# Two edits to a fused attention and two-MLP kernel: the activation's coefficients handled in the planned order, and the last output rows in two halves

## The chip, the core and the metric

The kernel runs as one program on one core of a Trainium2 chip. The time of a run is the device time in microseconds (us). Five engines work side by side, each through its own queue in order: TensorE (PE, whose weight loads are listed as PEld), VectorE (DVE), ScalarE (ACT), GpSimd (POOL) and SyncE (SP), which here only issues DMAs. A DMA can also be issued from ACT's queue. An instruction that has to wait holds up everything behind it on its engine.

## The reference, cut to what matters

Attention over 2 batches of 768 positions with 8 heads of 64 (a window of 16 around each position, plus one summary key and value for each block of 32), then two MLPs over the 1536 rows:

```python
# attention -> x [1536, 512]
h = x @ w_in                       # [1536, 2048]
P = a[0] + a[1]*h + a[2]*h*h + a[3]*h*h*h
Q = 1.0 + abs(b[0])*abs(h) + abs(b[1])*h*h
x = (P / (Q + 1e-6)) @ w_out       # first MLP, [1536, 512]
h = x @ w_in2
out = (h * cos(h)) @ w_out2        # second MLP, [1536, 512]
```

`a` has four numbers and `b` two. They are needed by the first MLP's activation alone.

## The kernel before, in words

The 1536 rows are twelve attention units of 128 rows; the MLPs work on three tiles T of 512 rows. The 2048 hidden features are sixteen slices f of 128. A unit of MLP work is one (layer, f, T): `mlp_h` makes 128 hidden features of 512 rows in PSUM with 12 matmuls (every fp32 factor is split in a high and a low part, three products each), `ew1` or `ew2` is the activation on ACT, DVE and POOL, `split_g` writes its high part gh and low part gl, and `mlp_o` adds gh and gl times the slice of the output weights into four PSUM accumulators `acc0` to `acc3`, 12 matmuls again. The very first tile is worked in halves of 256 rows, so its matmuls have 256 columns. Weights arrive as 64-bit floats and are unpacked by `conv` on DVE and POOL.

Nearly all work is recorded with `P.op(options, reads, writes, function)`: each option is an engine letter (A, V, P, T, S for SP's DMAs) with an assumed cost. `Plan.order` then lays all ops out in one order, with those costs, the buffers and due times that it works out backwards, and picks the engine where an op has several options. What is written by hand stands in `setup()`, which runs ahead of the plan: the identity, eight matmuls that warm TensorE up, and the coefficients. These come with two DMAs on ACT's queue (L391, L392), in which each of 128 partitions gets its own copy of 4 or 2 numbers; three operations on ACT (L394, L396, L397) and four on DVE (L395, L398, L399, L401), in turn, then make the square root of |b[1]| in `co[:, 8:9]`.

The start of the plan is batch 0's keys (`k_pair`, eight DMAs at L478, eight transposed tiles `ktp`, each copied by ACT at L360 and reduced to block maxima by DVE at L495), two loads of q (L583), three of v (L531, tile `big`, summed by POOL or DVE at L538), and the scores `sp` (L650), on which the softmax on DVE (L664) and ACT (L668) follows. The program gives a DMA one of eight completion semaphores in turn; a DMA waits until the one that had its semaphore before has landed. With the two loads of the coefficients in the turn, the seventh and eighth load of k wait for the first and second.

At the end of the program the unit of the second MLP's last slice for T = 2 runs `mlp_o`, where the loop over d = 0..3 makes 128 rows of the output each: three matmuls of 512 columns into `acc`d (L943), a copy to SBUF by ACT, a DMA on SP's queue (L978).

Of the kernel before, what the change touches and what calls it, by code (L numbers as in the profile page):

```python
# [13 lines left out]
ACTF = mybir.ActivationFunctionType  # L14
ALU = mybir.AluOpType
# [275 lines left out]
def kernel(  # L291
# [13 lines left out]
    nc = tc.nc  # L305
    B, NH, S, D = q.shape
# [10 lines left out]
    TT = 512  # L317
# [20 lines left out]
    P = Plan()  # L338
# [19 lines left out]
    def cp(e, o, i):  # L358
        if e == "A":
            nc.scalar.copy(out=o, in_=i)  # L360
        elif e == "P":
            nc.gpsimd.tensor_scalar(out=o, in0=i, scalar1=1.0, scalar2=1.0, op0=ALU.mult,  # L362
                                    op1=ALU.mult)
        else:
            nc.vector.tensor_copy(o, i)
# [4 lines left out]
    co = co_r.t  # L370
# [14 lines left out]
    def setup():  # L385
        make_identity(nc, ident)

        wu = pools["pa"].tile([128, 512], F32, tag="acc0", name="warm", bufs=1)
        for i in range(8):
            nc.tensor.matmul(out=wu[:, 0:128], lhsT=ident, rhs=ident, start=True, stop=True)  # L390
        nc.scalar.dma_start(out=co[:, 0:4], in_=moe_a.partition_broadcast(128))  # L391
        nc.scalar.dma_start(out=co[:, 4:6], in_=moe_b.partition_broadcast(128))  # L392

        nc.scalar.activation(out=co[:, 7:8], in_=co[:, 5:6], func=ACTF.Abs)  # L394
        nc.vector.tensor_scalar(out=co[:, 8:9], in0=co[:, 7:8], scalar1=1e-30, scalar2=None, op0=ALU.max)  # L395
        nc.scalar.activation(out=co[:, 8:9], in_=co[:, 8:9], func=ACTF.Ln)  # L396
        nc.scalar.activation(out=co[:, 8:9], in_=co[:, 8:9], func=ACTF.Exp, scale=0.5)  # L397
        nc.vector.reciprocal(out=co[:, 9:10], in_=co[:, 8:9])  # L398
        nc.vector.scalar_tensor_tensor(out=co[:, 9:10], in0=co[:, 9:10], scalar=co[:, 7:8],  # L399
                                       in1=co[:, 8:9], op0=ALU.mult, op1=ALU.add)  # L400
        nc.vector.tensor_scalar(out=co[:, 8:9], in0=co[:, 9:10], scalar1=0.5, scalar2=None, op0=ALU.mult)  # L401
        nc.gpsimd.memset(vsel, 0.0)

        nc.gpsimd.memset(vsel[:, 16:24], 1.0 / 32.0)
        nc.gpsimd.affine_select(out=vsel[:, 16:24], in_=vsel[:, 16:24], pattern=[[-16, 8]],
                                compare_op=ALU.is_ge, fill=0.0, base=0, channel_multiplier=1)
        nc.gpsimd.affine_select(out=vsel[:, 16:24], in_=vsel[:, 16:24], pattern=[[16, 8]],
                                compare_op=ALU.is_ge, fill=0.0, base=15, channel_multiplier=-1)
        for offs in masks:
            m = masks[offs].t  # L410
            nc.gpsimd.memset(m, 0.0)
            nc.gpsimd.memset(m[:, WK:KW], LN32_8)
            for half in range(2):
                off = offs[half]
                mh = m[64 * half:64 * half + 64, 0:WK]

                nc.gpsimd.affine_select(
                    out=mh, in_=mh, pattern=[[-1, WK]], compare_op=ALU.is_ge,
                    fill=NEG, base=off + 15, channel_multiplier=1)
                nc.gpsimd.affine_select(  # L420
                    out=mh, in_=mh, pattern=[[1, WK]], compare_op=ALU.is_ge,
                    fill=NEG, base=15 - off, channel_multiplier=-1)

    spare = [0]

# [421 lines left out]
    def ew1(un):  # L847
        n = un.n
# [1 line left out]
        te, tu, tf = (tmp(x) for x in ("te", "tu", "tf"))  # L850
        H, EE, U, Z = (lambda r=r: r.t[:, 0:n] for r in (h, te, tu, tf))

        P.op([("A", act(n, True, 1))], [], [h, tu],
             lambda e: nc.scalar.activation(out=U(), in_=H(), func=ACTF.Square, scale=b1s))
        P.op([("A", act(n, True, 1))], [], [h, tf],
             lambda e: nc.scalar.activation(out=Z(), in_=H(), func=ACTF.Abs, scale=b0))  # L856
        P.op([("A", act(n, True, 2)), ("V", dve(n, 2))], [], [h, te],
             lambda e: (nc.scalar.activation(out=EE(), in_=H(), func=ACTF.Identity, scale=a3, bias=a2)
                        if e == "A" else
                        nc.vector.tensor_scalar(out=EE(), in0=H(), scalar1=a3, scalar2=a2,  # L860
# [51 lines left out]
    def mlp_o(un):  # L912
# [15 lines left out]
        for d in range(4):  # L928
# [19 lines left out]
            if un.first and have:  # L948


                sl = (lambda pr=pr, d=d: pr.t[:, d]) if un.T < 2 else (lambda pr=pr, d=d: pr.t[:, 0, d])
                P.op([("A", act(512)), ("V", dvef(512))], [pr[d]], [ac],
                     lambda e, ac=ac, sl=sl: cp(e, ac.t, sl()))
            P.op([("T", 3 * MM * n / 512)], [w["h"], w["l"], un.gh, un.gl], [ac], mm)
            P.now += 3 * MM * n / 512
            if not un.spill:
# [21 lines left out]
                     lambda e, r0=r0, sl=sl: nc.sync.dma_start(out=out[r0:r0 + 128, :], in_=sl()))  # L978
        if un.spill and un.last:
            partial.pop(key, None)  # L980


    segs = []
# [53 lines left out]
    def run_fill(upto):  # L1037
        while state["i"] < min(upto, len(fill)):
            fn, *a = fill[state["i"]]
            state["i"] += 1  # L1040
            fn(*a)
# [32 lines left out]
            prio += 6.0  # L1074

    run_fill(need[1])
    run_conv(-1, P.now)
    run_fill(pos_need[0])
    n = len(units)
# [45 lines left out]
```

## Time and profile before

| what | value |
|---|---|
| median of 3 runs | 620.85 us (620.59 to 621.9) |
| the profiled execution's own time | 618.5 us |
| its span | 616.8 us |
| PE busy | 595.5 us, 97% of the span |
| DVE, ACT, POOL busy | 477.8, 396.4, 413.7 us |
| DMA | 51.8 MB, mean 84 GB/s |

The span runs from the first instruction to the last. "Busy" is what an engine's instructions took; of a group, "idle before" is the time that its engine stood still ahead of it, with the instruction or DMA that ended the wait. PEclk is TensorE's granted clock as a share of 2.4 GHz: over half of a stretch at 0.5 (1.2 GHz) shows as a number between.

### The profile page before, as it was taken

How to read it: one execution, taken by the hardware profiler on the slowest of the kernel's cores; microseconds unless marked ns; L12 is line 12 of the kernel's file. 1: busy time of each engine (PE TensorE's matmuls, PEld its weight loads, DVE VectorE, ACT ScalarE, POOL GpSimd, SP SyncE). 2: the span in 40 equal slices, each digit the busy share in tenths (PEclk: the TensorE clock that was granted, in tenths of full speed). 3: DMA queues.
4: the chain of work that ended last, by engine and by line, in shares of the span. 5: the costliest groups of instructions: out<-in, count | busy, mean ns of one | idle time of the engine just before them, and what ended most of it. 6: DMA issues, size and time to landing. Idle time of an engine off the chain costs nothing.

```text
span 616.8 us, 9933 instructions
## 1 busy us (share of the span) xinstructions
PE 595.5 (97%) x3516; PEld 489.9 (79%) x3516; DVE 477.8 (77%) x919; ACT 396.4 (64%) x842; POOL 413.7 (67%) x409
## 2 busy tenths in 40 slices
PE   8778997999999999999999999999999999999997
PEld 7467876787888888888888878888888888888886
DVE  3999887758899989999999899569656875773541
ACT  5988799668767666786677656455455446544553
POOL 4487984657987878789868777568446754574332
PEclk9989999899999999999999999999999999999999
DMA  8986963100221222112122124213201330000112
GB/s 247 261 231 161 251 181 103 27 1 35 69 69 35 69 69 69 55 59 94 34 73 77 57 71 136 67 41 102 98 28 41 104 102 2 34 1 1 69 51 86
DMA packets 68714, 51.80 MB, mean 84 GB/s; under 512 B 37288, under 2 KB 62888, under 8 KB 68664
## 3 DMA queue, kind: packets, MB, share of 16 engines
q1 hardware_dynamic: 68376, 51.16, 28.0%
q8 instruction: 28, 0.46, 0.3%
q14 instruction: 22, 0.18, 0.1%
q10 hardware_dynamic: 288, 0.00, 0.0%
HBM read 47.71 MB, written 3.15 MB: 82 GB/s over the span
## 4 chain that ended last, share of the span: by engine, by line
PE 61%; DVE 20%; ACT 9%; POOL 4%; issue 3%; DMA 3%; SPq 0%; DVEq 0%; ACTq 0%; POOLq 0%
PE acc L943 29%; PE h L820 28%; ACT sc L668 2%; DVE te L868 2%; DVE tu L876 2%; DVE h L879 2%; DVE te L866 2%; DVE te L882 2%; DVE f L784 2%; DVE f L788 2%; DVE f L780 2%; ACT h L874 1%; PE avp L742 1%; POOL tu L864 1%; DMA big<-in_v_dram 1%
## 5 line engine op out<-in xcount | busy, mean ns | idle before, releaser
L820 PE MATMUL h<-xH,w 128*128 128x512 f32 (+1 forms) x544 | 172.8, 380 | 3.3 <-ACT pt L360 2.2
L839 POOL TENSOR_TENSOR gl<-te,gh 128x512 fp32r<-128x512 f32 (+1 forms) x100 | 135.0, 1350 | 7.4 <-ACT gh L360 0.9
L362 POOL TENSOR_SCALAR gh<-te 128x512 fp32r<-128x512 f32 (+1 forms) x84 | 59.3, 706 | 100.9 <-DVE te L906 80.9
L943 PE MATMUL acc<-gh,w 128*128 128x512 f32 (+1 forms) x416 | 123.5, 380 | 1.3 <-POOL gh L362 1.3
L820 PEld LDWEIGHTS h<-xH,w 128*128 128x128 f32 x544 | 100.9, 189 | 23.4 <-ACT pt L360 2.7
L943 PE MATMUL acc<-w,gh 128*128 128x512 f32 x384 | 118.4, 389 | 0.4 <-DVE xL L965 0.4
L820 PE MATMUL h<-xL,w 128*128 128x512 f32 (+1 forms) x272 | 103.0, 379 | 0.1
L898 DVE SCALAR_TENSOR_TENSOR h<-tu,h 128x512 f32<-128x512 int32 x96 | 66.4, 691 | 36.0 <-ACT te L360 34.9
L820 PE MATMUL h<-big,w 128*128 128x512 f32 x384 | 92.1, 389 | 0.9 <-DVE te L882 0.9
L943 PEld LDWEIGHTS acc<-gh,w 128*128 128x128 f32 x416 | 76.2, 190 | 16.6 <-POOL gh L362 1.5
L794 POOL TENSOR_TENSOR w<-f,w 128x512 fp32r<-128x512 f32 x62 | 84.2, 1360 | 6.2 <-ACT w L360 3.9
L820 PEld LDWEIGHTS h<-big,w 128*128 128x128 f32 x384 | 72.0, 188 | 16.3 <-DVE te L882 1.4
L943 PEld LDWEIGHTS acc<-w,gh 128*128 128x128 f32 x384 | 72.0, 188 | 15.8 <-DVE xL L965 0.9
L864 POOL TENSOR_TENSOR tu<-tu,tf 128x512 f32<-128x512 f32 (+1 forms) x52 | 67.1, 1291 | 19.6 <-ACT tf L856 19.5
L943 PE MATMUL acc<-gl,w 128*128 128x512 f32 (+1 forms) x208 | 78.3, 377 | 0.2 <-POOL gl L839 0.2
L943 PE MATMUL acc<-w,gl 128*128 128x512 f32 x192 | 74.7, 389 | 0.0
L901 ACT ACTIVATE h<-h 128x512 f32<-128x512 f32 x48 | 27.9, 582 | 60.4 <-DVE h L898 60.4
L906 DVE TENSOR_TENSOR te<-te,h 128x512 f32<-128x512 f32 x48 | 32.9, 685 | 35.1 <-ACT h L903 34.9
L820 PEld LDWEIGHTS h<-xL,w 128*128 128x128 f32 x272 | 51.3, 189 | 9.4 <-DVE xL L753 0.3
L893 ACT ACTIVATE tu<-h 128x512 int32<-128x512 f32 x48 | 28.7, 598 | 45.7 <-PE h L820 45.7
L784 DVE SCALAR_TENSOR_TENSOR f<-raw,f 128x512 int32<-128x512 int32 x64 | 56.1, 877 | 0.5
L788 DVE SCALAR_TENSOR_TENSOR f<-raw,f 128x512 int32<-128x512 int32 x64 | 56.0, 875 | 0.6
(100 smaller groups left out, 974.7 us busy)
## 6 DMA issues: line engine op xcount, KB each, us to landing
raw<-in_moe_w_in_dram SPq DMA_DIRECT2D x32, 512.0 KB, 3.7
raw<-in_moe_w_out_dram SPq DMA_DIRECT2D x32, 512.0 KB, 3.3
vw<-in_v_dram SPq DMA_DIRECT2D x24, 192.0 KB, 4.7
qk<-in_q_dram SPq DMA_DIRECT2D x10, 256.0 KB, 3.8
out_dram<-part SPq DMA_DIRECT2D x8, 256.0 KB, 2.0
part<-in_k_dram SPq DMA_DIRECT2D x8, 192.0 KB, 4.6
big<-in_v_dram SPq DMA_DIRECT2D x3, 512.0 KB
qk<-in_k_dram SPq DMA_DIRECT2D x6, 256.0 KB, 3.3
```

Source lines behind the costliest of these rows:

```text
L362: nc.gpsimd.tensor_scalar(out=o, in0=i, scalar1=1.0, scalar2=1.0, op0=ALU.mult, op1=ALU.mult)
L784: lambda e, lohi=lohi, ft=ft: nc.vector.scalar_tensor_tensor(out=ft.t.bitcast(I32), in0=lohi()[1], scalar=-0x40000000, in1=ft.t.bitcast(I3 ...
L788: lambda e, lohi=lohi, ft=ft: nc.vector.scalar_tensor_tensor(out=ft.t.bitcast(I32), in0=lohi()[0], scalar=29, in1=ft.t.bitcast(I32), op0=A ...
L794: lambda e, ft=ft, w=w: E[e].tensor_tensor(out=w.t[:, 1, :], in0=ft.t, in1=w.t[:, 0, :].bitcast(F32), op=ALU.subtract),
L820: nc.tensor.matmul(out=h.t[:, 0:n], lhsT=lt, rhs=rt[:, kk, cs], start=(k0 == 0 and i == 0), stop=(k0 == 2 and i == 5))
L839: lambda e: E[e].tensor_tensor(out=un.gl.t[:, 0:n], in0=g.t[:, 0:n], in1=un.gh.t[:, 0:n].bitcast(F32), op=ALU.subtract))
L864: lambda e: E[e].tensor_tensor(out=U(), in0=U(), in1=Z(), op=ALU.add))
L893: lambda e: nc.scalar.activation(out=K().bitcast(I32), in_=H(), func=ACTF.Identity, scale=1.0 / (2.0 * math.pi)))
L898: lambda e, c=c: nc.vector.scalar_tensor_tensor(out=H(), in0=K().bitcast(I32), scalar=-c, in1=H(), op0=ALU.mult, op1=ALU.add))
L901: lambda e: nc.scalar.activation(out=H(), in_=H(), func=ACTF.Abs))
L906: lambda e: nc.vector.tensor_tensor(out=S_(), in0=S_(), in1=H(), op=ALU.mult))
L943: nc.tensor.matmul(out=dst, lhsT=lt, rhs=rt, start=(un.start and not have and i == 0), stop=(un.stop and i == 2), skip_group_check=have)
```

## The change

The two loads and seven small operations leave `setup()` and become planned ops in a new function `coefficients()`, called behind the ops of the first two attention units and ahead of the first weights. They all write one resource, `co_r`, so they keep their order among themselves, and the first three operations of `ew1` now read it. The loads go through SP's queue. In `mlp_o` the last 128 rows (the last unit, d = 3) branch to a new function `mlp_end`: three matmuls on columns 0 to 255 of the accumulator, a copy by ACT and a DMA on ACT's queue; then three on columns 256 to 511, a copy by DVE and a DMA on SP's queue. Both halves name the same accumulator `ac` as what they write.

```diff
@@ setup
-        nc.scalar.dma_start(out=co[:, 0:4], in_=moe_a.partition_broadcast(128))
-        nc.scalar.dma_start(out=co[:, 4:6], in_=moe_b.partition_broadcast(128))
-
-        nc.scalar.activation(out=co[:, 7:8], in_=co[:, 5:6], func=ACTF.Abs)
-        nc.vector.tensor_scalar(out=co[:, 8:9], in0=co[:, 7:8], scalar1=1e-30, scalar2=None, op0=ALU.max)
...
+    def coefficients():
+        P.op([("S", 0.1)], [], [co_r], lambda e: nc.sync.dma_start(out=co[:, 0:4], in_=moe_a.partition_broadcast(128)))
+        P.op([("S", 0.1)], [], [co_r], lambda e: nc.sync.dma_start(out=co[:, 4:6], in_=moe_b.partition_broadcast(128)))
+
+        P.op([("A", 0.2)], [], [co_r],
+             lambda e: nc.scalar.activation(out=co[:, 7:8], in_=co[:, 5:6], func=ACTF.Abs))
+        P.op([("V", 0.1)], [], [co_r],
+             lambda e: nc.vector.tensor_scalar(out=co[:, 8:9], in0=co[:, 7:8], scalar1=1e-30, scalar2=None,
+                                               op0=ALU.max))
...
@@ ew1
-        P.op([("A", act(n, True, 1))], [], [h, tu],
+        P.op([("A", act(n, True, 1))], [co_r], [h, tu],
...
@@ mlp_o
+            if un.last and un.l and un is units[-1] and d == 3:
+                mlp_end(un, w, ac, pr[d] if have else None, pr)
+                continue
...
+    def mlp_end(un, w, ac, res, pr):
+
+        for x, (e0, q) in enumerate((("A", nc.scalar), ("V", nc.sync))):
+            c = slice(256 * x, 256 * x + 256)
+
+            def mm(e, c=c):
+                gh, gl = un.gh.t[:, 384:512], un.gl.t[:, 384:512]
+                for i, (lt, rt) in enumerate(((gh, w.t[:, 0, c]), (gh, w.t[:, 1, c]), (gl, w.t[:, 0, c]))):
+                    nc.tensor.matmul(out=ac.t[:, c], lhsT=lt, rhs=rt, start=False, stop=i == 2,
+                                     skip_group_check=True)
+
+            P.op([("T", 0.35)], [w["h"], w["l"], un.gh, un.gl], [ac], mm)
+            P.now += 0.35
+            sl = (lambda c=c: pr.t[:, 3, c]) if un.T < 2 else (lambda c=c: pr.t[:, 0, 3, c])
+            P.op([(e0, 0.3)], [ac], [res[x]], lambda e, c=c, sl=sl: cp(e, sl(), ac.t[:, c]))
+            r0 = TT * un.T + 384
+            P.op([("S", 0.4)], [res[x]], [],
+                 lambda e, c=c, sl=sl, q=q, r0=r0: q.dma_start(out=out[r0:r0 + 128, c], in_=sl()))
...
@@ the plan's start
     run_fill(need[1])
+    coefficients()
     run_conv(-1, P.now)
```

The planner lays everything out anew, so the order of the attention stretch changes as well. From some way into the first MLP on the order is that of before, up to the last rows. Three places follow; in the changed kernel, a line L of the code above it stands 10 to 13 further on.

SP's queue at the start of the program, before, from the loads of v on (`vw` are windows of v, `qk` a tile of q, `raw` the weights):

```order
L531 DMA big<-in_v_dram 128x8x128 x3
L730 DMA vw_108<-in_v_dram 96x8x64
L730 DMA vw_109<-in_v_dram 96x8x64
L439 DMA qk<-in_q_dram 128x8x64
L439 DMA raw<-in_moe_w_in_dram 128x4x128
L730 DMA vw_110<-in_v_dram 96x8x64
L730 DMA vw_111<-in_v_dram 96x8x64
L550 DMA vw_110<-vw_108 24x512
L550 DMA vw_111<-vw_108 24x512
L439 DMA raw<-in_moe_w_out_dram 128x512
```

The same queue now:

```order
L541 DMA big<-in_v_dram 128x8x128 x3
L414 DMA co<-in_moe_a_dram 128x4
L740 DMA vw_108<-in_v_dram 96x8x64
L740 DMA vw_109<-in_v_dram 96x8x64
L449 DMA qk<-in_q_dram 128x8x64
L449 DMA raw<-in_moe_w_in_dram 128x4x128
L740 DMA vw_110<-in_v_dram 96x8x64
L740 DMA vw_111<-in_v_dram 96x8x64
L560 DMA vw_110<-vw_108 24x512
L560 DMA vw_111<-vw_108 24x512
L415 DMA co<-in_moe_b_dram 128x2
L449 DMA raw<-in_moe_w_out_dram 128x512
```

And ACT's queue now, where the coefficients' three operations come, in the softmax of the third unit (`sc`, `su`), with the first cast of a weight (`w`) ahead of them:

```order
L678 ACTIVATE sc,su<-sc,mn 128x120 x3
L360 CAST w_483<-f 128x512
L418 ACTIVATE co<-co 128x1
L360 CAST xH_112<-avp 128x4x128
L360 COPY pt<-ptp 120x512
L423 ACTIVATE co<-co 128x1
L678 ACTIVATE sc,su<-sc,mn 128x120
L425 ACTIVATE co<-co 128x1
```

The load of `a` stands behind the three loads of v, that of `b` behind the two small copies of `vw`, and none is on ACT's queue; ACT's queue no longer begins with the coefficients.

TensorE's queue between the first two groups of hidden features and the first products with output weights, before (`ptp`, `qtp`, `ktp` are transposes, `sp` scores, `avp` attention times values; the left-out rows are the other rows of one set of 16 `sp`):

```order
L820 MATMUL h<-xH_112,w_594 128x256
L695 MATMUL ptp<-ident,sc 120x128 x4
L601 MATMUL qtp<-ident,qk 128x128 x4
...
L943 MATMUL acc_739<-gh,w_567 128x256 x2
L943 MATMUL acc_739<-gl,w_567 128x256
```

The same stretch now; left out are 16 `sp`, then 16 `sp` and 16 `avp`, then the other rows of a group of 12 `h`:

```order
L830 MATMUL h<-xH_112,w_596 128x256
L611 MATMUL qtp<-ident,qk 128x128 x8
L523 MATMUL ktp<-ident,qk 128x128 x4
...
L705 MATMUL ptp<-ident,sc 120x128 x8
...
L830 MATMUL h<-xH_112,w_744 128x256
...
L953 MATMUL acc_850<-gh,w_543 128x256 x2
L953 MATMUL acc_850<-gl,w_543 128x256
```

Between the second `h` and the first `acc` there were one `ptp`, one `qtp` and one set of `sp`; now there are two of each, a `ktp`, a set of `avp` and a third group of `h`.

TensorE's last rows now, with what each waits for (`Activation` is a semaphore that ACT counts up):

```order
L953 MATMUL acc_6213<-w_5851,gh 128x512 x2
L953 MATMUL acc_6213<-w_5851,gl 128x512
L1003 MATMUL acc_6218<-w_5851,gh 128x256 x2
L1003 MATMUL acc_6218<-w_5851,gl 128x256
L1003 MATMUL acc_6218<-w_5851,gh 128x256 [waits Activation_49]
L1003 MATMUL acc_6218<-w_5851,gh 128x256
L1003 MATMUL acc_6218<-w_5851,gl 128x256
```

The three matmuls of 512 columns have become twice three of 256, and the fourth of them waits for ACT's count of 750, which is ACT's last operation: the copy of the first half out of the same accumulator.

## Rows read from the trace of the kernel before

**Rows 1.** The page's first part: busy us, share of the span, instructions of each engine.

```profile
PE 595.5 (97%) x3516; PEld 489.9 (79%) x3516; DVE 477.8 (77%) x919; ACT 396.4 (64%) x842; POOL 413.7 (67%) x409
```

**Rows 2.** Busy time by stretch: engines, then TensorE's clock, DMA share, GB/s.

```profile
35.00:45.00 10.00, 6.94 (x68) 5.82 (x66) 8.81 (x41) 8.01 (x32) 9.30 (x11) 0.83 0.80 233
...
55.00:65.00 10.00, 8.34 (x93) 7.89 (x93) 9.97 (x26) 9.16 (x26) 7.54 (x10) 1.00 0.54 151
...
400.00:600.00 200.00, 200.00 (x884) 165.58 (x884) 128.85 (x184) 104.05 (x189) 109.92 (x105) 1.00 0.16 50
```

**Rows 3.** Timeline of the first 26 us: start, duration, engine, line, idle before.

```profile
0.83 0.43 ACTq L391 DMA_DIRECT2D co<-in_moe_a_dram  x1
1.29 0.49 ACTq L392 DMA_DIRECT2D co<-in_moe_b_dram  x1
...
5.13 6.11 PE L487 MATMUL ktp<-ident,part 128*64 128x128 f32 x96
...
6.22 1.95 PEld L487 LDWEIGHTS ktp<-ident,part 128*64 128x64 f32 x36 [0.17 <-DMA part<-in_k_dram]
6.38 0.20 ACT L394 ACTIVATE co<-co 128x1 f32<-128x1 f32 x1 [4.30 <-DMA co<-in_moe_b_dram]
...
7.80 3.90 DVE L495 TENSOR_REDUCE big<-ktp 128x12 f32<-128x384 f32 x7
...
13.47 1.05 PE L650 MATMUL sp<-kw,qT 64*64 64x120 f32 x32 [0.39 <-ACT kw L360]
...
14.91 0.69 DVE L538 TENSOR_TENSOR big<-big 128x512 f32<-128x512 f32 x1 [1.88 <-DMA big<-in_v_dram]
15.52 0.28 DVE L664 CUSTOM_DVE_ANT_0 sc<-sp,mask 128x120 f32<-128x120 f32 x1
...
19.98 1.65 SPq L550 DMA_DIRECT2D vw<-vw  x2
...
24.46 0.19 ACT L668 ACTIVATION_READ_ACCUMULATOR sc<-sc,mn 128x1 f32 x1
```

**Rows 4.** By stretch as in rows 2: the first loads.

```profile
2.00:5.40 3.40, 3.40 (x18) 3.17 (x18) 0.00 (x0) 0.08 (x1) 2.76 (x13) 1.00 0.54 139
...
8.00:15.00 7.00, 6.61 (x154) 5.49 (x150) 4.06 (x9) 5.50 (x13) 2.10 (x2) 1.00 1.10 326
```

**Rows 5.** By stretch, the instructions on tile co alone: DVE and ACT busy.

```profile
6.00:8.00 2.00, 0.69 (x4) 0.61 (x3) 1.00 1.08 359
```

**Rows 6.** TensorE's timeline from 34 to 41 us: waits in brackets.

```profile
35.89 0.66 PE L601 MATMUL qtp<-ident,qk 128*128 128x128 f32 x4 [0.73 <-ACT pt L360]
37.33 1.05 PE L650 MATMUL sp<-kw,qT 64*64 64x120 f32 x32 [0.78 <-DVE qT L365]
39.70 0.64 PE L943 MATMUL acc<-gh,w 128*128 128x256 f32 x2 [1.32 <-POOL gh L362]
```

**Rows 7.** Timeline of the last 5 us.

```profile
611.98 0.41 PEld L943 LDWEIGHTS acc<-w,gh 128*128 128x128 f32 x2
612.20 0.62 PE L943 MATMUL acc<-w,gh 128*128 128x512 f32 x2
...
613.08 0.58 ACT L360 COPY big<-acc 128x512 f32<-128x512 f32 x1
...
613.69 0.33 SPq L978 DMA_DIRECT2D out_dram<-big  x1
```

**Rows 8.** SP's waits in the last 12 us: us in total, times, longest.

```profile
SPq L1120 <- DMA out_dram<-big: 1.7, 1, 1.7
```

**Rows 9.** TensorE's timeline: matmuls of 256 columns that follow each other without a wait.

```profile
46.37 0.40 PE L820 MATMUL h<-xH,w 128*128 128x256 f32 x2
46.61 0.28 PE L820 MATMUL h<-xL,w 128*128 128x256 f32 x1
```

**Rows 10.** Groups by shape: count, busy us, mean ns of one, idle before.

```profile
L360 ACT COPY big<-ktp 128x384 f32<-128x384 f32 x8 | 3.6, 477 | 0.8 <-PE ktp L487 0.7
...
L866 DVE TENSOR_TENSOR te<-te,h 128x256 f32<-128x256 f32 x8 | 3.3, 409 | 1.2 <-ACT te L858 1.2
```

More of the change, by code (lines that the diff above doesn't have):

```diff
@@ L390, in setup @@
             nc.tensor.matmul(out=wu[:, 0:128], lhsT=ident, rhs=ident, start=True, stop=True)
-        nc.scalar.dma_start(out=co[:, 0:4], in_=moe_a.partition_broadcast(128))
-        nc.scalar.dma_start(out=co[:, 4:6], in_=moe_b.partition_broadcast(128))
-        nc.scalar.activation(out=co[:, 7:8], in_=co[:, 5:6], func=ACTF.Abs)
-        nc.vector.tensor_scalar(out=co[:, 8:9], in0=co[:, 7:8], scalar1=1e-30, scalar2=None, op0=ALU.max)
[L396 to L401, printed above, removed]
         nc.gpsimd.memset(vsel, 0.0)
@@ L422, in setup @@
                     fill=NEG, base=15 - off, channel_multiplier=-1)
+    def coefficients():
[6 more added lines that the diff above has]
+                                               op0=ALU.max))
+        P.op([("A", 0.2)], [], [co_r],
+             lambda e: nc.scalar.activation(out=co[:, 8:9], in_=co[:, 8:9], func=ACTF.Ln))
+        P.op([("A", 0.2)], [], [co_r],
+             lambda e: nc.scalar.activation(out=co[:, 8:9], in_=co[:, 8:9], func=ACTF.Exp, scale=0.5))
+        P.op([("V", 0.1)], [], [co_r], lambda e: nc.vector.reciprocal(out=co[:, 9:10], in_=co[:, 8:9]))
+        P.op([("V", 0.1)], [], [co_r],
+             lambda e: nc.vector.scalar_tensor_tensor(out=co[:, 9:10], in0=co[:, 9:10], scalar=co[:, 7:8],
+                                                      in1=co[:, 8:9], op0=ALU.mult, op1=ALU.add))
+        P.op([("V", 0.1)], [], [co_r],
+             lambda e: nc.vector.tensor_scalar(out=co[:, 8:9], in0=co[:, 9:10], scalar1=0.5, scalar2=None,
+                                               op0=ALU.mult))
     spare = [0]
@@ L851, in ew1 @@
         H, EE, U, Z = (lambda r=r: r.t[:, 0:n] for r in (h, te, tu, tf))
-        P.op([("A", act(n, True, 1))], [], [h, tu],
+        P.op([("A", act(n, True, 1))], [co_r], [h, tu],
              lambda e: nc.scalar.activation(out=U(), in_=H(), func=ACTF.Square, scale=b1s))
-        P.op([("A", act(n, True, 1))], [], [h, tf],
+        P.op([("A", act(n, True, 1))], [co_r], [h, tf],
              lambda e: nc.scalar.activation(out=Z(), in_=H(), func=ACTF.Abs, scale=b0))
-        P.op([("A", act(n, True, 2)), ("V", dve(n, 2))], [], [h, te],
+        P.op([("A", act(n, True, 2)), ("V", dve(n, 2))], [co_r], [h, te],
              lambda e: (nc.scalar.activation(out=EE(), in_=H(), func=ACTF.Identity, scale=a3, bias=a2)
```

## The prediction, made before the changed kernel was run

> **What bounds the kernel now.** I read the page's busy times first: TensorE works 97% of the span [rows 1], so the question is where its other 3% lie. The busy times by stretch answer it. From 400 to 600 us TensorE is busy for 200.00 of 200 us [rows 2]: nothing that another engine does better there can shorten the run. In the attention stretch it is not: 6.94 of 10 us from 35 to 45, 8.34 from 55 to 65, while DVE has 9.97 there [rows 2]. So up to about 65 us the time is set by DVE and ACT and by what they wait for, later by TensorE, and at the very end by the chain last matmul, copy, DMA. A microsecond won at the start is kept if DVE and ACT pass it on; one lost in the tail is lost whole. The reader then goes to the timeline of the start, of 34 to 41 us, and of the last 5 us.
>
> All sums are made against the profiled execution (618.5 us, span 616.8); the median of the timed runs is 620.85, 2.35 us above it, so I add the same difference to both.
>
> **Part 1, the start.** ACT stands still for 4.30 us until the load of `b` has landed; its first operation on the coefficients is at 6.38 [rows 3]. The copies of `ktp` and with them DVE's first reduction (7.80 [rows 3]) stand behind. That is the visible stall. The one that sets the end of the start is another: the softmax of the first unit on DVE (15.52) stands behind a sum of v at 14.91, which waited 1.88 us for its load [rows 3]. The scores that it needs ran at 13.47 to 14.52. So taking away ACT's stall alone would move little: DVE would wait for v just as long. What matters is whether v comes earlier.
>
> The loads move 139 GB/s from 2.0 to 5.4 us at a DMA share of 0.54, and 326 GB/s from 8 to 15 us at 1.10 [rows 4]. The slow stretch is the one in which the coefficients' two loads are under way, issued at 0.83 and 1.29 and done by 6.38 [rows 3]. I take them as its cause: many tiny packets on a second queue, alternating with those of k. If k had run at 326 GB/s from 2.0 on, 3.4 us would have moved 3.4 x (326 - 139) = 636 KB more, which is 1.95 us of the later rate. The second load of v, which DVE waits for at 14.91, would land at about 13.0. The other limit is the transposes of k: 36 weight loads take 1.95 us [rows 3], 54 ns each, so 96 take 5.2 us where they now take 6.11 from 5.13 on [rows 3], held up by DVE's late reductions; the scores could end some 0.7 to 0.9 us earlier, at 13.7. The sum of v then runs from 13.0 to 13.7, the scores end at the same time, and the softmax begins at about 13.9 in place of 15.52: **-1.6 us**. Bounds: 0 if the loads are no faster (a cold start, rival A), -1.95 if only v counts.
>
> The Trainium skill speaks against my reading. "DMA: Bandwidth & Descriptors", section "Why small descriptors are slow (HBM only)", gives a small packet a fixed overhead of about 3 cycles and 32 bytes of metadata, no more; by that a few hundred tiny packets would be nothing, and the start would gain 0 in place of 1.6 us, which makes this rival A. The same page, "Issuing engines are not separate DMA queues", says that loads from ACT's and SP's queues share the same 16 engines and interleave, which is what my reading needs. Rows 4 show the halved rate, not its cause.
>
> **Part 2, the coefficients in their new place.** Their four operations on DVE take 0.69 us and the three on ACT 0.61 [rows 5]. Before, they fell into time in which DVE had nothing else to do. Now they stand in the softmax of the third unit, where DVE is near 10 of 10 us; the two engines work side by side, so I count DVE's alone: **+0.7 us** (0.6 to 1.3 if both count). The loads sit in SP's queue past which the windows of v, a tile of q and the first weights must go; if each costs the loads behind it half of the 1.95 us above, that only takes back the lead that the loads have by then, and DVE and ACT are the slower side there.
>
> A new wait: ACT now meets the first operation on `b` behind the softmax of the second unit and one cast. Before, that softmax ended at 24.65 [rows 3]; with a cast of about 0.5 that is 25.1. The load of `b` is issued behind the copies of `vw`, which end at 21.63 [rows 3]. From issue to use it took 6.38 - 1.29 = 5.1 us at the start [rows 3], beside k. So it is there between 21.63 + 2.0 (1.7 us of SP's last wait [rows 8] and its 0.33 of issue [rows 7], for a DMA alone) and 26.7: ACT waits 0 to 1.6 us, with its own cast of x, a transposed probability and the third unit's exponentials behind it, and DVE and TensorE behind these. Both places move up alike when the start is faster. I take **+0.3**, nearer to the idle DMA since the two copies ahead are small.
>
> **Part 3, the new order.** In 34 to 41 us TensorE waits 0.73, 0.78 and 1.32 us [rows 6], 2.8 in sum, ahead of the first products with output weights, and then runs at half clock: 0.83 over 10 us [rows 2] is 3.4 us at 1.2 GHz, worth 1.7. The order now puts a second `qtp` and `ptp` group, a `ktp`, a second set of `sp`, a set of `avp` and 12 `h` in that place, which is work enough to fill it (12 `h` of 256 columns alone are 12 x 0.12 = 1.4 us [rows 9], a set of `sp` 1.05 [rows 3]). If its inputs are ready, both go: -4.5. But DVE and ACT make those inputs, and where they are full a wait only moves. So I take about half of the waits and none of the clock, **-1.5**. On the other side, one more such gap with its stretch at half clock would cost 2.8 + 1.7 minus what it brings, some +3.
>
> **Part 4, the last 128 rows.** The order decides this one: the second half's first matmul waits for ACT's copy of the first half, since both name one accumulator. The halves run one after the other. Before, the last three matmuls begin at 612.20, the copy is at 613.08 to 613.66, the DMA at 613.69 [rows 7]. Now: three matmuls of 256 columns, 0.12 apart and 0.28 long [rows 9], 612.20 to 612.72; ACT is busy with the copy before until about 613.0 (the last now begins at 613.08); its half copy takes 0.37 (0.48 for 384 columns [rows 10], 0.58 for 512 [rows 7], so 0.8 ns a column), to 613.4; the weight load leads a matmul by 0.22 [rows 7], so the second half runs from 613.65 to 614.17; DVE's copy of 256 columns takes 0.41 [rows 10], to 614.6; the DMA is issued 0.9 later than before. It carries half the bytes, of which the 1.7 us of landing [rows 8] may give back 0 to 0.3. ACT's own DMA is long done. **+0.8** (0.5 to 1.0). Without the wait the split would have brought -0.2 to -0.4.
>
> Here a rule of the skill bears on the wait: "PSUM — Partial Sum Buffer", section on bank collisions, says that two engines must not touch one PSUM bank at once, whatever the columns. By it the wait isn't a slip that a finer dependency could take away: halves of one bank have to take turns. The order agrees; no run here shows it yet.
>
> **Sum.** -1.6 + 0.7 + 0.3 - 1.5 + 0.8 = -1.3: 617.2 for the profiled execution, **619.5** for the median. The rest of the program (200.00 of 200 us [rows 2]) keeps its order and its time.
>
> **Rivals.**
> - **A, the slow first loads are a cold start.** For it: the rate is low from the first packet on, and the coefficients are a few KB. Against it: it lasts just as long as their loads. Then the start gains nothing (v still lands at 14.9), the coefficients cost their 0.7 + 0.3 in a full stretch, the tail 0.8, and of the order's 1.5 little remains, since the plan's lead is missing: 620.85 + 1.8 = 622.6. It decides as soon as DVE's first softmax stands later than 15 us. Chance 0.18.
> - **B, given back.** The start is faster, but ACT's wait for `b` is near its upper end of 1.6, or the new order only moves TensorE's waits: -1.6 + 0.7 + 0.3 + 0.8, and 0 for part 3, is +0.2; with half of part 3, -0.6. 620.2 to 621.1. For it: DVE's 9.97 of 10. Chance 0.27.
> - **C, another gap.** The new order opens a gap before or behind, long enough for one more stretch at 1.2 GHz: +3.2, 624. The stretch at 0.83 [rows 2], behind waits of only 2.8 us in sum, shows that TensorE is close to that edge. Chance 0.08.
> - **D, the gap closes whole:** part 3 at -4.5: 616.5. Chance 0.07.
>
> My forecast has 0.40. A measurement of this kernel tells 0.2% (1.24 us) from no change. Faster: forecast and D, 0.47. Same: B, 0.27. Slower: A and C, 0.26. The range that leaves out D and C, and reaches the price of A, is 616.9 to 622.6; the forecast's own is 618.0 to 619.6, so a good part of it lies near the bound.
>
> **What would show it.** Right: no wait for coefficients ahead of ACT's first copy; over 250 GB/s between 2 and 5.4 us; DVE's first softmax at 13.6 to 14.2; the coefficients' first ACT operation with a wait under 0.7; TensorE's waits ahead of its first `acc` under 1.5 us in sum and a clock above 0.83; the last DMA 0.7 to 1.0 us later after the start of the last d than before (1.49). Wrong: a first stretch still at 140 GB/s (A), over 1 us of ACT's time in front of the load of `b`, a third stretch at half clock, or the two halves side by side.

## The result, and the profile after

The changed kernel takes 628.5 us (median of four: 625.61, 627.86, 629.15, 629.58), where the kernel before took 620.72 (618.05 to 621.9). The ratio is 1.0125, 95% interval 1.0088 to 1.0163: slower by about 8 us, outside my range and on the other side of my forecast. The profiled execution after has a span of 623.9 us (own time 625.61), 7.1 more than before, so the profile shows most of the loss, not all.

The first part of the page and TensorE's slices, after:

```profile
PE 599.7 (96%) x3519; PEld 493.5 (79%) x3519; DVE 482.5 (77%) x917; ACT 399.1 (64%) x848; POOL 409.5 (66%) x406
...
PEclk9879999899999999999999999999999999999999
```

Against [rows 1] TensorE is busy for 4.2 us more, with the same matmuls but for the tail's, and idle for 2.9 us more (24.2 against 21.3). Busy time that grows without new work points to the clock. The stretches that answer to [rows 2, 4], after, in the same columns:

```profile
2.00:5.40 3.40, 3.40 (x18) 3.17 (x18) 0.00 (x0) 0.08 (x1) 2.76 (x13) 1.00 0.94 254
8.00:15.00 7.00, 6.61 (x167) 6.14 (x164) 4.77 (x8) 5.64 (x13) 2.06 (x2) 1.00 1.14 326
25.00:35.00 10.00, 6.45 (x79) 5.22 (x78) 8.30 (x30) 7.56 (x28) 5.20 (x6) 0.66 1.09 316
35.00:45.00 10.00, 6.63 (x67) 5.82 (x65) 9.96 (x34) 8.75 (x32) 6.99 (x8) 0.83 0.87 226
55.00:65.00 10.00, 7.88 (x108) 6.78 (x107) 9.96 (x32) 9.04 (x30) 9.05 (x11) 1.00 0.44 120
...
400.00:600.00 200.00, 200.00 (x884) 165.61 (x883) 129.54 (x186) 102.86 (x186) 111.71 (x107) 1.00 0.16 51
```

The first loads run at 254 GB/s where they ran at 139 [rows 4]: that step is right. But 35 to 45 us is no fuller than before (6.63 against 6.94), 55 to 65 is emptier, and 25 to 35 has a clock of 0.66: 6.8 us at 1.2 GHz that the kernel before does not have, as its row shows:

```profile
25.00:35.00 10.00, 8.14 (x118) 6.81 (x114) 9.65 (x38) 9.70 (x34) 5.22 (x5) 1.00 1.08 286
```

TensorE's timeline there, after (start, duration, engine, line, operation, count, idle before):

```profile
24.63 0.65 PE L705 MATMUL ptp<-ident,sc 128*120 128x128 f32 x4
27.50 0.65 PE L705 MATMUL ptp<-ident,sc 128*120 128x128 f32 x4 [2.22 <-POOL sc L691]
29.48 1.11 PE L611 MATMUL qtp<-ident,qk 128*128 128x128 f32 x4 [1.33 <-DMA qk<-in_q_dram]
30.52 1.98 PE L752 MATMUL avp<-pt,vw 120*64 120x64 f32 x32
...
38.10 0.63 PE L611 MATMUL qtp<-ident,qk 128*128 128x128 f32 x4 [0.45 <-PE h L830]
41.53 0.80 PE L611 MATMUL qtp<-ident,qk 128*128 128x128 f32 x3 [2.81 <-ACT qT L360]
```

Before, the same two waits, for POOL's `sc` and for the tile of q, were under 1 us each:

```profile
26.95 0.65 PE L695 MATMUL ptp<-ident,sc 128*120 128x128 f32 x4 [0.91 <-POOL sc L681]
28.44 0.66 PE L601 MATMUL qtp<-ident,qk 128*128 128x128 f32 x4 [0.84 <-DMA qk<-in_q_dram]
```

After, TensorE is almost idle from 25.2 to 29.5, and what follows runs slow: `avp` takes 1.98 us for its 32 matmuls, 1.15 at full clock. Then the work that I took for a filler, a second `qtp` group next to the first, waits 2.81 us for ACT's copy of the first: the gap of [rows 6] has only changed its name.

The start, after, DVE's rows that answer to [rows 3]:

```profile
7.24 0.56 DVE L505 TENSOR_REDUCE big<-ktp 128x12 f32<-128x384 f32 x1 [7.24 <-ACT big L360]
...
13.49 0.93 DVE L548 TENSOR_TENSOR big<-big 128x512 f32<-128x512 f32 x1
15.21 0.28 DVE L674 CUSTOM_DVE_ANT_0 sc<-sp,mask 128x120 f32<-128x120 f32 x1 [0.80 <-PE sp L660]
```

The sum of v is 1.42 us earlier and waits for no load; the first softmax is only 0.31 us earlier, held by the scores. And the tail, after, answering to [rows 7]:

```profile
618.84 0.40 PE L1003 MATMUL acc<-w,gh 128*128 128x256 f32 x2
619.07 0.28 PE L1003 MATMUL acc<-w,gl 128*128 128x256 f32 x1
...
619.95 0.50 PE L1003 MATMUL acc<-w,gh 128*128 128x256 f32 x2 [0.60 <-ACT big L360]
620.29 0.28 PE L1003 MATMUL acc<-w,gl 128*128 128x256 f32 x1
620.67 0.42 DVE L365 COPY big<-acc 128x256 f32<-128x256 f32 x1 [7.28 <-PE acc L1003]
621.12 0.33 SPq L1012 DMA_DIRECT2D out_dram<-big  x1
```

From the start of the last d to the last DMA issue it is 2.28 us, before 1.49: +0.79; I had worked out 0.9. To the end of the span it is 5.06 against 4.60: half the bytes land sooner, so +0.46 net. The last d starts 6.64 us later than before, so the loss lies ahead of the tail. The last of the twelve `avp` groups tells how far ahead; before, then after:

```profile
130.55 1.15 PE L742 MATMUL avp<-pt,vw 120*64 120x64 f32 x32
```

```profile
136.36 1.15 PE L752 MATMUL avp<-pt,vw 120*64 120x64 f32 x32
```

5.8 us of the 7.1 are there when attention ends. Up to the end of this group TensorE stands still for 19.1 us after and 16.2 before; from there to 400 us for 1.1 and 1.4.

### The profile page after: what moved, and what is told of

Its sections match the earlier page's. It is cut to its first block, busy times and chain, and to the rows that moved or that the text cites. A ratio compares the mean times of both kernels' runs of the same rounds, so it can differ in the third digit from the quotient of the medians.

```text
span 623.9 us, 9951 instructions
## 1 busy us (share of the span) xinstructions
PE 599.7 (96%) x3519; PEld 493.5 (79%) x3519; DVE 482.5 (77%) x917; ACT 399.1 (64%) x848; POOL 409.5 (66%) x406
## 4 chain that ended last, share of the span: by engine, by line
PE 61%; DVE 24%; ACT 8%; issue 3%; POOL 2%; DMA 1%; SPq 0%; DVEq 0%; ACTq 0%; POOLq 0%
PE h L830 28%; PE acc L953 27%; DVE tu L886 3%; DVE te L892 3%; DVE h L889 3%; DVE f L794 3%; DVE f L798 2%; DVE te L878 2%; DVE te L876 2%; DVE f L790 1%; ACT sc L678 1%; ACT h L884 1%; PE sp L660 1%; DMA qk<-in_q_dram 1%; DVE sc L674 1%
## 5 line engine op out<-in xcount | busy, mean ns | idle before, releaser
L362 POOL TENSOR_SCALAR gh<-te 128x512 fp32r<-128x512 f32 (+1 forms) x80 | 56.2, 702 | 99.2 <-DVE te L916 81.1
L362 POOL TENSOR_SCALAR w<-f 128x512 fp32r<-128x512 f32 x45 | 29.1, 649 | 43.0 <-DVE f L798 28.2
L794 DVE SCALAR_TENSOR_TENSOR f<-raw,f 128x512 int32<-128x512 int32 x64 | 56.8, 889 | 0.6
```

Of the source, the lines that this page charges most:

```text
L794: lambda e, lohi=lohi, ft=ft: nc.vector.scalar_tensor_tensor(out=ft.t.bitcast(I32), in0=lohi()[1], scalar=-0x40000000, in1=ft.t.bitcast(I3 ...
```

## The experiments

Timed runs stand beside runs of the kernel before on the same chip; a ratio below 1 is faster.

**Which part loses?** Each part alone. The split tail on the kernel before (`e1_tail`):

```diff
+            if un.last and un.l and un is units[-1] and d == 3:
+                mlp_end(un, w, ac, pr[d] if have else None, pr)
+                continue
```

> The kernel before with the split tail alone. By my own term for the tail (the second half waits for ACT's copy of the first) it is 0.5 to 0.8 us slower than the kernel before, about 621.4; the last DMA is issued some 2.3 us after the start of the last d, where it was 1.49. If the two halves ran side by side it would be 0.2 to 0.4 us faster. No theory of the attention stretch expects a change here: if this kernel loses several microseconds, either the tail holds much more of the loss than its trace shows or the loss comes and goes by chance.

619.29 us against 619.39, ratio 0.9997 (0.9983 to 1.0012). Its trace has the same 2.28 us to the last DMA (613.42 to 615.70) and 5.08 to the end. The tail's half microsecond is in the trace, below what the timing resolves.

The new order with the coefficients where they were (`e2_order`): loads and operations stand in setup as before, and the nine planned operations keep their prices but do nothing.

```diff
+        nc.scalar.dma_start(out=co[:, 0:4], in_=moe_a.partition_broadcast(128))
...
     def coefficients():
-        P.op([("S", 0.1)], [], [co_r], lambda e: nc.sync.dma_start(...))
+        for e, c in (("S", 0.1), ("S", 0.1), ("A", 0.2), ("V", 0.1), ("A", 0.2), ("A", 0.2), ("V", 0.1), ("V", 0.1), ("V", 0.1)):
+            P.op([(e, c)], [], [co_r], lambda e: None)
```

> The changed kernel's order of the attention stretch to the last instruction, but with the coefficients loaded and prepared at the start on ACT's queue as before, and with the old tail. Theory L (the load of b, in SP's queue ahead of the third tile of q, holds that tile up and so opens the gap at 25 to 29.5 us): the gap goes, the time is within 1.2 us of the kernel before, 620 to 622. Theory O (the re-planned order itself opens the gaps): still 625 to 628, with TensorE nearly idle at 25 to 29.5 us and three stretches at half clock. Theory C (chance: when the clock rises at the start decides): the time follows the moment of the rise in the first 8 us, whatever the loads and the order.

628.16 us, ratio 1.0138 (1.0112 to 1.0163). The new order alone carries the whole loss; theory L falls. In the traces this kernel and the changed one run the same operations in the same order on all four compute engines, coefficients and tail apart. "Order" includes the planner's choice of engines: 848 operations on ACT where before has 842, and three fewer each on DVE and POOL. Theory C falls with this trace: its transposes of k end at 11.3 us, before at 11.2, so TensorE got up to speed no later, and it still takes 626.5. The wait for the tile of q and the low clock are there without any load of b (25 to 35 us in this run):

```profile
28.68 0.65 PE L700 MATMUL ptp<-ident,sc 128*120 128x128 f32 x4 [2.40 <-POOL sc L686]
30.53 1.12 PE L606 MATMUL qtp<-ident,qk 128*128 128x128 f32 x4 [1.20 <-DMA qk<-in_q_dram]
```

The coefficients moved in before's order (`e3_loads`): a new function puts them into the finished list, a behind v, b behind the copies of `vw`, the operations around the first cast of x.

```diff
+    order = put(order)
```

> The kernel before in its own order, with only the coefficients moved: a on SP's queue behind v, b on SP's queue behind the two copies of vw and ahead of the raw weights and the third tile of q, their operations on ACT and DVE at the first cast of x; old tail. Theory L: the third tile of q lands late and the time is 625 to 628. Theory O: the start gains what the changed kernel's start gained or more (0.3 to 1.6 us), the operations cost 0.7, so 619.5 to 621.2. Theory C: follows the clock's rise.

620.79 us, ratio 1.0020 (1.0002 to 1.0038): near theory O's upper end. Its order on the four engines is that of before, coefficients apart. The first softmax is at 13.74 here, 1.78 us earlier than before, yet nothing comes of it: TensorE then waits for the tile of q, and 0.66 is the mean clock from 25 to 35 us here too.

```profile
29.03 1.12 PE L613 MATMUL qtp<-ident,qk 128*128 128x128 f32 x4 [2.62 <-DMA qk<-in_q_dram]
```

The changed kernel with the old tail (`e4_coef`, without the three lines of the first diff):

> The changed kernel with the old tail: moved coefficients and the new order together. The tail's share being 0.5 to 0.8 us, all theories of the attention stretch expect 627.7 to 628.0 here; theory C alone allows a time near 621 in some of the runs.

627.28 us, ratio 1.0134 (1.0107 to 1.0160). So 628.2 for the order, 627.3 with moved coefficients, 620.8 for these alone. The profiled run of `e4_coef` tells two things apart. It has the full clock from 25 to 35 us, with the same order:

```profile
25.00:35.00 10.00, 6.69 (x96) 5.66 (x96) 9.40 (x26) 9.00 (x33) 5.58 (x7) 1.00 1.06 292
```

Its span is 621.5 us, 4.7 above before, and of these 4.0 are TensorE standing still (25.3 against 21.3). So waits of 3 to 4 us come with the order in all three traces that have it (24.2 in the changed kernel, 25.5 in `e2_order`); the stretch of 6.8 us at 1.2 GHz came in two of the three.

**Is it this order, or any other?** Two orders that have nothing to do with the change (`p1_plan`, `p2_plan`): one constant of the planner by 1% or so.

```diff
-SPT = 1.2
+SPT = 1.19
```

> The kernel before with nothing but the planner's price of a set of sp changed from 1.2 to 1.19 us, so that the planner finds another order from the fourth unit on (its own estimate is 2.9 us shorter). Theory R (before's order is a picked one, and nearly any re-planning of the attention stretch loses several microseconds): 622 to 628. Theory S (the order that came with the coefficients is a bad draw, others scatter about the kernel before): 617 to 621.

624.32 us, ratio 1.0077 (1.0055 to 1.0099): theory R.

```diff
-    return n / 960.0 + 0.068 + 0.06 * aps
+    return n / 960.0 + 0.069 + 0.06 * aps
```

> The kernel before with the planner's fixed price of a DVE instruction at 0.069 instead of 0.068 us; its order differs from before's from some 75 us on (its own estimate is 2.2 us shorter). Theory R (before's order is a picked one): slower again, 621.5 to 627. Theory S: within 2 us of the kernel before, to either side. Should it be equal or faster, the planner's re-ordering hurts only where it falls in the first 60 us, with idle time on TensorE.

620.53 us, ratio 1.0034 (1.0016 to 1.0053). This is 1.6 us above before, below theory R's range and inside theory S's. Both are slower, although the planner took both for shorter; the one that leaves before's order later loses less. So three new orders out of three are slower, which is a small sample, and only two by the several microseconds of theory R. Why before's order is the better one these runs don't show.

**Where in the order?** Repairs by hand. First the tile of q alone in the kernel before (`f2_qearly`): its load and two of raw weights go ahead of the copies of `vw`.

```diff
+    on = [i for i, o in enumerate(order) if o.eng == "S"]
+    for x in (21, 22, 23):
+        o = order.pop(on[x])
+        order.insert(on[19] + x - 21, o)
```

> The kernel before, with three loads on SP's queue (two of raw weights, the fourth tile of q) moved ahead of the two copies of vw, behind which they wait for work of TensorE until 21.6 us. TensorE's wait of 0.84 us for that tile at 28.44 goes. If the tile is what holds up the chain at 26 to 30 us, 0.5 to 1 us faster; if DVE's full stretch sets the time anyway (9.65 of 10 us busy at 25 to 35), no change, 619.4.

618.68 us, ratio 1.0000 (0.9983 to 1.0017). The wait for the tile goes (`qtp` at 27.77 without one), the time stays: in before's order that wait cost nothing that the timing can tell. The same move in the changed kernel, and POOL's normalising ahead of a subtraction of weights (`g2_repair`):

```diff
+    for x in (23, 24, 25):
+        o = order.pop(on[x])
+        order.insert(on[20] + x - 23, o)
+    nth = [i for i in onp if order[i].opts[0] == ("P", 0.95)][3]
+    order.insert(nth, order.pop(onp[onp.index(nth) - 1]))
```

> The changed kernel with the old tail and two repairs by hand in its order: on SP's queue the same three loads ahead of the copies of vw and of the load of b; on POOL the last normalising of sc of the second unit ahead of a subtraction of weights (1.27 us) behind which it stood. Theory O in the form 'two gaps': TensorE's waits of 2.2 us for sc and 1.3 us for the tile of q at 25 to 29.5 us shrink to under 1 us each, the half-clock stretch at 28 to 35 us goes, and 2 to 3.5 us of the 8 come back: 624 to 625.5. The rest (the second group of qtp that waits 2.8 us at 40 us, more waits from 85 to 125 us) stays. If the first gap has no part in the loss: 627 to 628.5.

628.14 us, ratio 1.0134 (1.0105 to 1.0162): no gain, and a mistake of mine. The load of b now stood behind three large loads, and ACT waited for it:

```profile
27.70 0.20 ACT L418 ACTIVATE co<-co 128x1 f32<-128x1 f32 x1 [2.62 <-DMA co<-in_moe_b_dram]
```

The same slip in the kernel before with moved coefficients (`g1_early`):

> The kernel before in its own order with the coefficients' loads and operations moved to SP's queue and into the attention stretch (as in the run with the moved loads alone, 620.8 us against 619.4), and in addition two loads of raw weights and the fourth tile of q ahead of the copies of vw and so ahead of the load of b. If the wait for that tile (2.6 us there, 0.8 before) is what turned the faster start into a loss, the wait and the half-clock stretch from 28 us go, the lead of about 1 us stays, and the time is 617.8 to 618.6. If the lead is taken back by DVE anyway: 619 to 620. Under 617.5 nothing here explains.

621.44 us, ratio 1.0028 (1.0011 to 1.0046), ACT waiting 0.50 us for b. Then both with b right behind a. The changed kernel with the loads alone mended (`h2_loads`):

```diff
+    s = [o for o in order if o.eng == "S"]
+    for x, y in ((22, 14), (23, 20), (24, 20), (25, 20)):
+        order.remove(s[x])
+        order.insert(order.index(s[y]), s[x])
```

> The changed kernel with the old tail and its own order on all compute engines, but with the load of b right behind a and the three loads ahead of the copies of vw. The wait of TensorE for the tile of q (1.3 us at 29 us) goes, ACT does not wait for b; the wait for POOL's sc (2.2 us at 27.5 us) stays. If the loads' order carries a good part of the loss: 625 to 626.5. If the order on the compute engines carries it: 627 to 628.5, as without the edit (627.3).

626.55 us, ratio 1.0107 (1.0082 to 1.0132), between the two ranges. And with POOL's two operations swapped as well (`h3_pool`):

> The same, and POOL's last normalising of sc of the second unit ahead of the subtraction of weights: the first gap on TensorE (25 to 29.5 us) is closed from both sides. If this gap with its half-clock stretch is 2 to 3.5 of the 8 us: 624 to 625.5, with a mean clock of 0.991 or more where it was 0.986. If the loss is spread over the whole attention stretch: 626.5 to 628.5.

625.85 us, ratio 1.0101 (1.0074 to 1.0127), again between the two. The two waits of the first gap are shorter here, no wait is above 1.08 us from 24 to 35 us, and the clock is full; but TensorE does no more work there than in `e4_coef` (6.69 us, 96 matmuls, also at full clock). 25 to 35 and 35 to 45 us of this run, and TensorE's second gap:

```profile
25.00:35.00 10.00, 6.67 (x93) 5.38 (x92) 9.64 (x29) 8.74 (x33) 6.04 (x6) 1.00 1.00 247
35.00:45.00 10.00, 6.43 (x59) 5.08 (x57) 8.45 (x35) 7.91 (x26) 8.40 (x9) 0.76 0.92 238
```

```profile
39.52 0.66 PE L611 MATMUL qtp<-ident,qk 128*128 128x128 f32 x4 [2.81 <-ACT qT L360]
```

The same row of `e4_coef`, without the repairs:

```profile
39.69 1.12 PE L611 MATMUL qtp<-ident,qk 128*128 128x128 f32 x4 [2.80 <-ACT qT L360]
```

The repairs bring TensorE to its second gap 0.17 us earlier, and the half clock now comes behind it (0.76 from 35 to 45 us, 0.66 from 55 to 65). In time, 627.28 against 625.85, the two kernels ran on different chips, the intervals overlap, and at a mean clock of 0.993 both have runs of 623 us. So what the first gap is worth is not shown; by these traces it is little. The larger part arises behind it. Where, the stretches of before, then after, show:

```profile
55.00:75.00 20.00, 18.34 (x173) 16.79 (x172) 18.77 (x44) 16.02 (x42) 16.37 (x20) 1.00 0.77 198
105.00:145.00 40.00, 38.00 (x307) 30.29 (x308) 27.91 (x75) 29.42 (x74) 23.66 (x23) 0.96 0.08 18
145.00:205.00 60.00, 59.06 (x261) 48.37 (x260) 54.91 (x83) 41.01 (x69) 51.81 (x45) 1.00 0.17 54
205.00:400.00 195.00, 194.56 (x857) 160.50 (x856) 177.10 (x258) 127.64 (x218) 153.17 (x135) 1.00 0.23 73
```

```profile
55.00:75.00 20.00, 16.64 (x172) 14.11 (x170) 19.96 (x53) 17.39 (x50) 15.64 (x19) 1.00 0.63 165
105.00:145.00 40.00, 36.82 (x328) 29.16 (x327) 26.22 (x81) 27.49 (x77) 22.75 (x23) 0.96 0.09 21
145.00:205.00 60.00, 60.00 (x267) 49.67 (x266) 55.23 (x81) 42.98 (x73) 49.50 (x44) 1.00 0.16 49
205.00:400.00 195.00, 193.88 (x851) 159.00 (x850) 180.41 (x263) 130.30 (x223) 151.77 (x133) 1.00 0.23 72
```

TensorE loses 1.7 us more from 55 to 75, where DVE is busy for 19.96 of 20, 1.2 more from 105 to 145, wins 0.9 to 205 and loses 0.7 more to 400. In the changed kernel the work comes up to 6 us later, so a stretch does not hold quite the same work in both; the 3 us more of standing still by the end of attention and none behind it, counted above, do not depend on that. There is no single wait to take out.

**What are the moved coefficients worth in before's order?** The operations alone, loads at the start as before (`h4_ops`, the list of `e3_loads` without its two loads):

> The kernel before in its own order, loads at the start on ACT's queue as before, and only the seven operations on the coefficients moved to the first cast of x. My term for them was +0.7 us (0.6 to 1.3), less what ACT's earlier start of the ktp copies gives: 619.4 to 620.2. If they lie beside other work: 618.5 to 619.4.

619.70 us against 619.45, ratio 1.0006 (0.9989 to 1.0022): +0.4 us by the ratio, -0.7 to +1.4 by its interval, so my 0.7 is neither shown nor ruled out. Loads and operations, b behind a, and the three loads early (`h1_best`):

```diff
-        for key, e, nth, more in (("a", "S", 13, 0), ("b", "S", 21, 0), ...
+        for key, e, nth, more in (("a", "S", 13, 0), ("b", "S", 13, 0), ...
+    for x, y in ((23, 21), (24, 21), (25, 21)):
```

> The kernel before in its own order, with the coefficients' operations moved to the first cast of x, both coefficient loads on SP's queue right behind v, and two loads of raw weights and the fourth tile of q ahead of the copies of vw. In the run that moved the three loads with b left behind the copies, ACT waited 0.5 us for b and the time was 621.4. If that wait and the late tile of q were the reasons why the moved loads did not pay, both are gone here and the time is 617.5 to 618.8 (before 619.0 to 619.4). If DVE and ACT take a faster start back in any case: 619.5 to 621.5.

618.59 us against 619.45, ratio 0.9992 (0.9975 to 1.0009). The lowest median, and no proven gain: with the order kept, the moved coefficients cost nothing and bring nothing that the timing can tell (-1.5 to +0.6 us). Its trace shows no lead at the start that could be passed on: the first softmax is at 15.51 us, before 15.52.

**The first loads.** One row to one partition, spread by a matmul with ones (`f1_onepkt`):

```diff
+        nc.scalar.dma_start(out=row[:, 0:4], in_=moe_a.partition_broadcast(1))
+                nc.tensor.matmul(out=wu[:, 128:134], lhsT=row[:, 8:136], rhs=row[:, 0:6], start=True, stop=True)
+        nc.scalar.copy(out=co[:, 0:6], in_=wu[:, 128:134])
```

> The kernel before in its own order; only the two coefficient loads at the start change: each fetches one row to one partition, and a matmul with a row of ones spreads it over the 128 partitions between the warm-up matmuls. If the many tiny packets are what holds the first loads at 139 GB/s, the rate from 2 to 5.4 us rises to about 254 GB/s as in the changed kernel, ACT has no wait of 4.3 us, and the scores of the first unit come 0.5 to 1.0 us earlier; the time falls by 0 to 1.0 us, 618.4 to 619.4, less if the fourth tile of q is then waited for instead. If the slow start is a cold start: same rate, same time.

621.05 us, ratio 1.0031 (1.0013 to 1.0049): slower, against every expectation. Half of it held; the stretches of this run and its sum of v:

```profile
2.00:5.40 3.40, 3.40 (x17) 3.15 (x16) 0.00 (x0) 0.08 (x1) 2.77 (x13) 1.00 0.92 249
8.00:15.00 7.00, 6.37 (x155) 5.62 (x152) 3.76 (x7) 5.63 (x13) 2.10 (x2) 1.00 1.05 280
```

```profile
15.74 0.69 DVE L543 TENSOR_TENSOR big<-big 128x512 f32<-128x512 f32 x1 [2.80 <-DMA big<-in_v_dram]
```

The tiny packets gone, k is loaded at 249 GB/s, at a DMA share of 0.92 where it was 0.54 [rows 4]: beside the tiny packets the DMA engines were not full, they stood still for nearly half the time. Both loads still take their turns among the eight semaphores here, so the turns are not the cause. But from 8 to 15 us the rate is 280 where it was 326, and v comes later than before. Why stays open. With the three loads early as well (`f3_both`):

> Both edits: the lead of the start is passed on because the tile of q no longer stops it. If both sizes hold, 1 to 2 us faster than the kernel before, 617.4 to 618.4, with the end of the last avp group at about 130 us where it was 131.7; if DVE or the clock takes it back, 619.4.

619.99 us against 619.30, ratio 1.0009 (0.9996 to 1.0022): no gain either.

**The tail's wait.** The second half in another PSUM tile, DVE adding the earlier sum (`g3_bank`):

```diff
+            to = psum([128, 512], "last") if x else ac
+                P.op([("V", 0.4)], [ac], [res[1]], lambda e: cp(e, sl1(), ac.t[:, 256:512]))
...
+                     lambda e, c=c, sl=sl, to=to: nc.vector.tensor_tensor(out=sl(), in0=to.t[:, c], in1=sl(), op=ALU.add))
```

> The split tail on the kernel before, with the second half of the last rows accumulated in another PSUM tile, so that its matmuls need not wait for ACT's copy of the first half (DVE has taken the earlier sum out of the bank before, and adds it at the end). If the shared accumulator is what made the split dear, the last DMA is issued 0.9 to 1.3 us after the start of the last d's matmuls (2.28 in the changed kernel, 1.49 in the kernel before) and the end comes 0.2 to 0.6 us earlier than before; too little for the clock on the wall, 618.8 to 619.4. If something else spaces the halves, 2 us or more remain.

619.74 us against 618.97, ratio 1.0005 (0.9982 to 1.0028), a tie. The halves now follow each other without a wait:

```profile
615.47 0.40 PE L997 MATMUL acc<-w,gh 128*128 128x256 f32 x2
615.70 0.28 PE L997 MATMUL acc<-w,gl 128*128 128x256 f32 x1
615.82 0.40 PE L997 MATMUL last<-w,gh 128*128 128x256 f32 x2
```

0.35 us apart instead of 1.11, and the last DMA is issued at 616.83, 1.36 after the first matmul. The shared accumulator was the price, as I had said. But the end is 4.63 us after that matmul, before 4.60: what the earlier issue wins (1.36 against 1.49), the landing of the two DMAs, issued 0.27 us apart, takes back. Splitting this tail wins nothing even without the wait.

## Why the prediction was wrong

**The step that failed is part 3**, the new order at -1.5 us. It measured +8.8 (`e2_order` against its own runs of before, 628.16 - 619.39), past even the +3 that I had as its other end. I priced one gap, that of [rows 6] at 34 to 41 us, and read the new order as filling it, since more work stood in the place. But an in-order engine is not filled by what stands in its list, only by what is ready: the second `qtp` waits 2.81 us for ACT, the `ptp` 2.22 for POOL. And the order changes all through the attention stretch, where TensorE stands still longer in several places, not in this one alone: 2.1 us more from 25 to 50 us, 0.7 from 50 to 75, 1.3 from there to the end of attention, against 1.2 less before 25. I had taken the other engines to set the time up to 65 us alone. I knew how full the other engines are: from 35 to 45 us DVE has 8.81 of 10 us, ACT 8.01, POOL 9.30 [rows 2], and now DVE has 9.96. I named DVE and ACT as what could hold TensorE up, not POOL, and still counted half of the waits as a gain. That the rest of the program keeps its time was right: behind attention TensorE stands still no longer than before (1.1 against 1.4 us up to 400). Which of the many re-ordered operations makes the waits stays open.

**Rival C** named the right kind of thing, a new gap with one more stretch at 1.2 GHz, at +3.2 and a chance of 0.08. Both are there at 25 to 35 us of the profiled run. The 6.8 us at 1.2 GHz account for at most 3.4 of its 7.1 us, TensorE's longer standing still for 2.9; and `e4_coef` loses 4.7 without that stretch. The chance should have been that of a whole re-planned order being worse.

**Part 1** was right in its mechanism and, in `e3_loads`, in its size: the sum of v at 13.13 us (I had 13.0), still behind a wait of 1.11 for its load, and the first softmax 1.78 us earlier (I had 1.6). In the changed kernel it was 0.31, in `e4_coef` 1.06 (14.46): the transposes of k ended at 10.2, 11.8 and 10.8 us in the three. In the changed kernel TensorE was slow there, not the loads: ACT's first copies of transposed tiles come 1.15 us apart, then 0.65 (at 6.73, 7.88 and 8.53), in `e3_loads` 0.65 from the first. One trace each is a thin measure: in the eight traces with the tiny loads at the start the first softmax is at 15.43 to 17.33 us, in the eight with them on SP's queue behind v at 13.74 to 15.69, 1.3 us earlier in the mean. The error is in passing it on. In `e3_loads` the lead ends in a wait of 2.62 us for the tile of q, and in none of the runs that keep before's order is a gain in time proven. The price that I weighed against it ("DMA: Bandwidth & Descriptors", "Why small descriptors are slow (HBM only)" in the Trainium skill: about 3 cycles a packet and 32 bytes of metadata), which I took for next to nothing, does not cover what `f1_onepkt` shows: without the tiny packets 249 GB/s at a share of 0.92, with them 142 at 0.56 in `f2_qearly` on the same chip.

**Part 2**: 0.66 us on DVE in the trace after, as predicted, but in before's order +0.4 us in time (`h4_ops`, interval -0.7 to +1.4). ACT's wait for b was 0 in the changed kernel; the price appeared when I pushed the load back (2.62).

**Part 4**: 0.9 to the last DMA issue, measured 0.79; 0.33 came back in the landing where I had let 0.1 come back, so +0.46 net in place of +0.8. The wait for ACT's copy was as predicted. That two engines must not be in one PSUM bank at once is what "PSUM — Partial Sum Buffer", "PSUM bank collisions raise a hardware error", in the Trainium skill says. `g3_bank` agrees as far as it goes: apart in two tiles the halves don't wait. In one tile the wait is the program's own, since both halves name `ac`, and no run leaves it out there.

Rival A (cold start) fell with the 254 GB/s. B and D did not come.

## What to carry to other kernels

When a planner sets the order, an edit that it sees can re-draw much of the order, far from the edit, and a shorter time by the planner's own costs is no promise: here three new orders of three were slower, by 0.3 to 1.4%, and it took two of them for shorter. Price that first, and keep the order fixed when an edit is to be judged (put the new instructions into the old list by hand). Where two engines are full, more work in a third engine's gap is no gain until you have named what makes it ready.

## What the runs showed of the hardware that I had not expected

- The time of one and the same kernel goes with its mean granted clock. The kernel before, over all comparisons: at 0.997 a mean of 617.85 us (17 runs), at 0.994 619.24 (59), at 0.989 621.37 (9); single runs overlap (617.80 to 621.99 at 0.994). The order made by the change ran at 0.985 to 0.988 in ten of its sixteen runs (changed kernel, `e2_order`, `e4_coef`), with a mean of 627.4, in four at 0.977 to 0.981, and in two above: 623.21 at 0.993 and 628.46 at 0.991. Against runs of before at almost the same clock (619.24 at 0.994, 620.09 at 0.991) the loss is 4 us by the one and 8 by the other, so these runs don't settle how much of it is the clock.
- A load of 1 KB in tiny packets is not quick behind large ones: in `g2_repair` b was issued at 23.36 and used at 27.70, 4.3 us later, and for the last 2.6 of them ACT waited for it.
- Two DMAs of half the size, issued 0.27 us apart, were followed by the end of the program 3.27 us after the last issue (`g3_bank`); one of full size 3.11 (before), one of half size behind an earlier one 2.78 (after).
